# Decay tables on ScalarE, states ahead of masks, rows ahead of weights: three reorderings in a fused RWKV-5 and top-1 routing kernel

## The chip, the cores and the metric

The kernel runs on one core of a Trainium2 chip. A core has TensorE (PE, with its weight loads shown apart as PEld), VectorE (DVE), ScalarE (ACT), GpSimd (POOL) and SyncE (SP), which here only issues DMA transfers. The engines run side by side and wait for each other by semaphores; each works through its own instructions in order. The metric is the device time of one execution in microseconds (us). The kernel before takes 476.0 us in the median of three runs (474.22 to 477.74). The profile is of one execution with a span of 475.0 us.

## The reference

An attention block with a decaying state feeds a mixture of experts with one expert per token.

```python
# r, k, v: (4, 8, 768, 48); w, u: (8, 48)
for t in range(S):
    cur = einsum('bhd,bhe->bhde', u * k[t], v[t])
    y[t] = einsum('bhd,bhde->bhe', r[t], state + cur)
    state = w[:, :, None] * state + einsum('bhd,bhe->bhde', k[t], v[t])
x = y.transpose(0, 2, 1, 3).reshape(3072, 384)
logits = x @ w_gate                       # (3072, 8)
expert = argmax(logits); gate = softmax(logits)[expert]
for e in range(8):                        # w1: (384, 1024), w2: (1024, 384) per expert
    out[mask] = gate * (relu(x[mask] @ w1[e]) @ w2[e])
```

## The kernel before

The attention is cut into 32 units: 4 batches, 2 halves of 384 positions (3 chunks of 128), 4 pairs of heads. With Wp holding the rising powers of w within a chunk and Wr the falling ones, a unit scales r and k by tables (W1 and W2, shifted by half a chunk so that the numbers stay near 1), forms the products of a chunk, puts u's term on the diagonal, masks the part above it, and adds the term of the state that the chunks before left. The states come from k scaled by Wg and v.

The powers are doubled step by step on VectorE, after some matmuls that keep TensorE busy:

```python
        warm = pool.tile([128, 128], FP32, name="warm")
        for i in range(WARM):
            nc.tensor.matmul(warm, lhsT=ident, rhs=ident, start=True, stop=True, skip_group_check=True)

# ... (ranges of w, seven doublings of Wp and Wr on VectorE)
```

The tables and the scaling of a unit:

```python
        def tables(h0, h1):
            hs = slice(h0, h1)
            by = bc(w_64[:, hs, None], [128, h1 - h0, C])
            nc.vector.tensor_tensor(W2[:, hs], Wr[:, hs], by, op=ALU.mult)
            nc.vector.tensor_tensor(W1[:, hs], Wp[:, hs], by, op=ALU.mult)

        # tables_g(h0, h1): W3 = Wr * pw[LV-1] on VectorE, turned on TensorE, copied to Wg by ACT
# ...
        def u_scale(u):
            x = units[u]
            hp = x["hp"]
            nc.gpsimd.tensor_tensor(x["RK"], x["r"], x["k"], op=ALU.mult)
            nc.gpsimd.tensor_tensor(x["K"], x["k"], bc(W2[:, hp, None, :], [128, HC, C]), op=ALU.mult)
            nc.vector.tensor_tensor(x["R"], x["r"], bc(W1[:, hp, None, :], [128, HC, C]), op=ALU.mult)

        def u_scale_g(u):
            x = units[u]
            hp, ns = x["hp"], x["ns"]
            nc.gpsimd.tensor_tensor(
                x["Kg"][:, 0:ns, :], x["kt"][:, 0:ns, :],
                bc(Wg[:, hp].rearrange("p h d -> p (h d)")[:, None, :], [128, ns, 2 * D]), op=ALU.mult)

```

Products, diagonal, mask, states and output of a unit. Gp is one PSUM buffer for all units, P has two per head of the pair:

```python
        def u_scores(u):
            x = units[u]
            hp, A = x["hp"], x["A"]
            P = x["P"] = [ps.tile([128, 512], FP32, name=f"P{hi}", tag=f"P{hi}", bufs=2) for hi in range(2)]
            for c in range(HC):
                for hi in range(2):
                    q = slice(64 * hi, 64 * hi + D)
                    o = HC * C + c
                    nc.tensor.matmul(P[hi][:, o:o + 1], lhsT=x["RK"][q, c, :],
                                     rhs=wu[q, 1, hp:hp + 1], start=True, stop=True, skip_group_check=True)
            for c in range(HC):
                for hi in range(2):
                    q = slice(64 * hi, 64 * hi + D)
                    nc.tensor.matmul(P[hi][:, c * C:(c + 1) * C], lhsT=x["K"][q, c, :], rhs=x["R"][q, c, :],
                                     start=True, stop=True, skip_group_check=True)
            dv = ca.tile([128, 2, HC], FP32, name="dv", bufs=2)
            for hi in range(2):
                nc.scalar.copy(dv[:, hi], P[hi][:, HC * C:HC * C + HC])
            for c in range(HC):
                for hi in range(2):
                    nc.scalar.activation(A[:, hi, c, :], ident, func=ACT.Copy, scale=dv[:, hi, c:c + 1])

        def u_mask(u):
            x = units[u]
            A, P = x["A"], x["P"]
            for hi in range(2):
                nc.vector.copy_predicated(
                    A[:, hi], bc(mask[:, None, :].bitcast(I32), [128, HC, C]),
                    P[hi][:, 0:HC * C].rearrange("p (c t) -> p c t", t=C))
# ...
        def u_state(u):
            x = units[u]
            St, hp = x["St"], x["hp"]
            for c in range(x["ns"]):
                for hi in range(2):
                    nc.tensor.matmul(Gp[64 * hi:64 * hi + D, c, hi, 0:D], lhsT=x["Kg"][:, c, hi * D:(hi + 1) * D],
                                     rhs=vh(x, c, hi, D), start=True, stop=True, skip_group_check=True)
            prev = units[u - HP]["St"][:, HC - 1] if x["hf"] else None
            for c in range(x["ns"]):
                if prev is None:
                    nc.vector.tensor_copy(St[:, c, :, 0:D], Gp[:, c, :, 0:D])
                else:
                    nc.vector.scalar_tensor_tensor(out=St[:, c, :, 0:D], in0=prev[:, :, 0:D],
                                                   scalar=wC[:, hp:hp + 1], in1=Gp[:, c, :, 0:D], ...)
                prev = St[:, c]
        # ... u_out: yp = states x R (L533) + V x A (L537); y copied by ACT (L540)
```

u_gate turns a half's outputs into rows of x and their logits (three chunks per half, one in each of three units). choose makes gate weights and the expert of each row of a batch; its last steps store the rows to x_hbm in HBM, from the SP queue. ranks, onehots and early work out where each row goes; early does so ahead of time for two full tiles of 128 rows of experts 0 and 1. These steps are spread over units by a list:

```python
        for b in range(B - 1):
            g = 2 * HP * (b + 1) + 2
            for i in range(4):
                todo[g + min(i, 1) + i // 3].append(lambda b=b, i=i: chosen[b][i]())
            for i, step in enumerate(R.ranks(b, "y") + R.onehots(b, 3)):
                todo[g + 3 + i].append(step)
            if b == NB - 1:
                mark, columns, index = R.early("y")
                todo[g + 6].append(mark)
                todo[g + 7].append(columns)
                todo[g + 9].append(index)
        tiles = [Tile(R, j, early=True) for j in range(NEARLY)] + [Tile(R, j) for j in range(NSURE - NEARLY)]
```

The main program. Loads of r, k, v are issued four units ahead from the SP queue; the first four experts' second weights and two first weights are loaded beside the units. The buffers of the units lie in the memory of the last four experts' second weights, so those are loaded when the units end:

```python
            tables(0, 1)
            u_scale(0)
            tables_g(0, HP)
            u_scores(0)
            tables(1, HP)
            u_scale(1)
            u_scale_g(0)
            u_scores(1)
            u_mask(0)
            u_state(0)
            u_scale_g(1)
            R.begin()
            gate_weights()
            for u in range(NU):
                if u + 4 < NU:
                    u_load(u + 4)
                if HP <= u < HP + 4 * NW:
                    w2_load((u - HP) // 4, u % 4, 4)
                elif HP + 4 * NW <= u < HP + 4 * NW + NEARLY * DT:
                    tiles[(u - HP - 4 * NW) // DT].load_w1(wp, (u - HP - 4 * NW) % DT)
                if u + 2 < NU:
                    u_scale(u + 2)
                    u_scale_g(u + 2)
                if u + 1 < NU:
                    if u:
                        u_scores(u + 1)
                    u_mask(u + 1)
                    u_state(u + 1)
                u_out(u)
                if u >= HP and u % HP < HC:
                    u_gate(u // HP - 1, u % HP, "rw")
                for step in todo[u]:
                    step()
                # ... gather of the early tiles in unit 28
            fr.close()
            for e in range(NW, E):
                w2_load(e)
            t0, t1, t2, t3 = tiles[0:4]
            t0.turn(la, "g")
            # ... rows of x of the last three chunks
            mo = em.enter_context(tc.tile_pool(name="mo", bufs=2))
            shift, first, weight, rest = chosen[B - 1]
            shift()
            t0.hidden(mo, 0)
            first()
            weight()
            rest()
            for step in R.ranks(B - 1, "rw"):
                step()
            t0.hidden(mo, 1)
            R.bases(rt)
            R.slots(rt)
            for u in range(NU, NU + HP):
                for step in todo[u]:
                    step()
            for step in R.onehots(B - 1):
                step()
            R.owners(rt)
            t2.load_w1(wp)
            t1.turn(la, "g")
            t0.result(mo)
            R.index(rt, "rw")
            t2.load_x(mo)
            t3.load_x(mo)
            t0.store()
            t1.hidden(mo, 0)
            t1.hidden(mo, 1)
            t3.load_w1(wp)
            t1.result(mo)
            t1.store()
            t2.turn(mo, "g")
```

A tile gathers 128 rows by index (xs), turns them on TensorE (xTp, copied to xT), multiplies by w1 of its expert (hp, with relu to hT) and by w2 (yp), scales by the gate weight (yo) and stores by index:

```python
        def turn(self, mo, tag):

            p = self.R.ps.tile([128, DT, 128], FP32, name="xTp", tag=tag, bufs=BUFS[tag])
            for d in range(DT):
                nc.tensor.transpose(p[:, d, :], self.xs[:, 128 * d:128 * d + 128], ident)
            self.xT = self.tile(mo, [128, DT, 128], "xT", 2)
            nc.vector.tensor_copy(self.xT, p)
        # ... hidden: hp = w1 x xT, relu to hT; result: yp = hT x w2, yo = yp * xs[:, DM:W]
```

run_tiles repeats this for 26 tiles, with rows two tiles and weights two tiles ahead. A general path for other values of w exists in the file and does not run here.

## Time and profile before

| engine | busy us | share of the span |
|---|---|---|
| PE | 443.7 | 93% |
| PEld | 371.7 | 78% |
| DVE | 151.5 | 32% |
| ACT | 125.8 | 26% |
| POOL | 159.7 | 34% |

DMA moved 95.45 MB, 201 GB/s over the span. The page of the profile begins with these totals. Its second part cuts the span into 40 slices: a digit is the busy share of an engine in tenths (9 is 90% or more), PEclk is the granted TensorE clock in tenths of full speed, DMA the mean busy share of the core's 16 DMA engines. Further views list who waited for whom (engine, line, what it waited for; total us, times, longest), the instructions in order of time with the idle time of their engine before them in brackets, and the busy time in chosen stretches. L512 is line 512 of the kernel's file. A wait for several semaphores is put down to the one that came last by the profile; where the engine named had long been done, it was another. A matmul of 32-bit numbers appears as two records.

Lines to know: L480 and L485 the diagonal's and the chunk's products (P), L489 and L492 the diagonal on ACT, L498 the mask, L512 the state matmuls (Gp), L517 and L519 the state updates out of Gp, L533 and L537 the output (yp), L459, L460 and L461 the scaled RK, K and R, L466 the scaled k for the states, L566 the rows of x (rp), L163 the store of rows, L886 the gather of a tile, L892 and L894 its turning, L905 and L914 its two products.

### The profile page before, as it was taken

Reading aid. Unit: us, or ns where it says so; the run is one execution under the profiler, and the core shown is the slowest. Engines: PE = TensorE matmul, PEld = TensorE weight load, DVE = VectorE, ACT = ScalarE, POOL = GpSimd, SP = SyncE. Lnnn points to the kernel's source line nnn. Section 1 sums busy time; section 2 is a strip of 40 time slices with the busy share of each in tenths; the row PEclk is TensorE's granted clock in tenths of the full one; section 3 lists DMA queues with packets and bytes.
Section 4 is the critical chain, followed back from the end, with each engine's and each line's share of the span. In section 5 each row is a group of like instructions: output and inputs, shape, how many; then the busy total and the mean of one; then the engine's idle time right before and its main releaser. Section 6 shows DMA issues by size and latency. Waiting matters only on the chain.

```text
span 475.0 us, 10408 instructions
## 1 busy us (share of the span) xinstructions
PE 443.7 (93%) x4138; PEld 371.7 (78%) x4138; DVE 151.5 (32%) x399; ACT 125.8 (26%) x376; POOL 159.7 (34%) x193
## 2 busy tenths in 40 slices
PE   4999989889979996999999999999999999999992
PEld 4888888878868876877777888887777788888871
DVE  7436785985886720110001100001000010000100
ACT  0557776656555210111111111111111111111110
POOL 7857773964852025111111222111111112211000
PEclk8569999999989998999999999999999999999997
DMA  6348859949927997555555445445555544445400
GB/s 234 118 133 271 282 170 305 397 176 336 400 97 245 369 340 179 192 182 193 199 205 183 164 166 184 162 174 177 183 185 199 203 170 151 179 171 180 155 17 14
DMA packets 24576, 95.45 MB, mean 201 GB/s; under 512 B 3840, under 2 KB 6950, under 8 KB 20676
## 3 DMA queue, kind: packets, MB, share of 16 engines
q1 hardware_dynamic: 20322, 83.40, 49.6%
q0 software_dynamic: 3904, 11.23, 8.3%
q8 instruction: 38, 0.62, 0.6%
q14 instruction: 22, 0.18, 0.1%
q10 hardware_dynamic: 290, 0.02, 0.0%
HBM read 85.18 MB, written 10.24 MB: 201 GB/s over the span
## 4 chain that ended last, share of the span: by engine, by line
issue 35%; PE 31%; POOL 6%; DMA 3%; DVE 2%; POOLq 0%; ACT 0%
PE hp L905 13%; PE yp L914 10%; POOL xs L886 3%; DMA w_all<-in_r_k_units_dram 2%; POOL out_dram L919 2%; PE rp L566 2%; DMA xs<-x_hbm,idx 2%; PE yp L537 2%; PE yp L533 1%; PE P L485 1%; PE P L480 1%; PE xTp L892 1%; PE Gp L512 1%; POOL w_all L459 0%; POOL w_all L460 0%
## 5 line engine op out<-in xcount | busy, mean ns | idle before, releaser
L905 PEld LDWEIGHTS hp<-xT,w1s 128*128 128x128 f32 x1344 | 155.8, 193 | 8.5 <-DVE xT L894 1.7
L905 PE MATMUL hp<-xT,w1s 128*128 128x128 f32 x1344 | 156.7, 277 | 1.3 <-DVE xT L894 1.3
L914 PE MATMUL yp<-w_all,hT 128*128 (+1 forms) x448 | 149.1, 486 | 0.0
L914 PEld LDWEIGHTS yp<-w_all,hT 128*128 128x128 f32 x448 | 82.9, 190 | 51.9
L907 ACT ACTIVATE hT<-hp 128x512 f32<-128x512 f32 x56 | 33.4, 597 | 268.9 <-PE hp L905 267.4
L919 POOL DMA_INDIRECT out_dram<-yo,idx x26 | 26.5, 1019 | 224.2 <-DVE yo L916 214.7
L492 ACT ACTIVATE A<-ident,dv 128x128 f32<-128x128 f32 x192 | 59.6, 389 | 0.2 <-ACT dv L489 0.2
L894 DVE COPY xT<-xTp 128x384 f32<-128x384 f32 x28 | 15.6, 557 | 132.3 <-PE xTp L892 132.3
L916 DVE TENSOR_SCALAR yo<-yp,xs 128x384 f32<-128x384 f32 x26 | 16.1, 618 | 125.1 <-PE yp L914 125.1
L459 POOL TENSOR_TENSOR w_all<-w_all 128x384 f32<-128x384 f32 x32 | 35.1, 1098 | 32.3 <-PE rkp L716 11.1
L498 DVE COPY_PREDICATED A<-mask,P 128x384 f32<-128x384 int32 x64 | 33.8, 582 | 36.0 <-ACT A L492 24.2
L537 PE MATMUL yp<-A,w_all 128*64 128x128 f32 x384 | 42.1, 293 | 0.0
L886 POOL DMA_INDIRECT xs<-x_hbm,idx x26 | 25.3, 973 | 36.2 <-ACT hT L907 28.5
L460 POOL TENSOR_TENSOR w_all<-w_all,W 128x384 f32<-128x384 f32 x32 | 34.8, 1087 | 2.7 <-PE P L485 1.4
L533 PE MATMUL yp<-w_all,St 128*64 128x128 f32 x320 | 34.5, 291 | 0.0
L485 PE MATMUL P<-w_all 48*128 48x128 f32 x384 | 32.3, 305 | 1.7 <-DVE w_all L461 1.4
L480 PEld LDWEIGHTS P<-wu,w_all 48*128 48x128 f32 x384 | 26.4, 204 | 6.5 <-POOL w_all L459 2.3
L480 PE MATMUL P<-wu,w_all 48*128 48x1 f32 x384 | 28.9, 262 | 1.6 <-POOL w_all L459 1.6
L461 DVE TENSOR_TENSOR w_all<-w_all,W 128x384 f32<-128x384 f32 x32 | 27.6, 862 | 2.5 <-DMA w_all<-in_r_k_units_dram 2.4
L485 PEld LDWEIGHTS P<-w_all 48*128 48x128 f32 x384 | 26.7, 206 | 2.1 <-POOL w_all L460 1.6
L537 PEld LDWEIGHTS yp<-A,w_all 128*64 128x64 f32 x384 | 26.9, 149 | 0.4 <-DVE A L498 0.4
L466 POOL TENSOR_TENSOR w_all<-w_all,Wg 128x288 f32<-128x288 f32 (+1 forms) x32 | 25.2, 788 | 2.8 <-ACT Wg L438 1.4
(127 smaller groups left out, 254.4 us busy)
## 6 DMA issues: line engine op xcount, KB each, us to landing
w1s<-in_moe_w_dram SPq DMA_DIRECT2D x26, 1536.0 KB, 6.5
w_all<-in_r_k_units_dram SPq DMA_DIRECT2D x32, 384.0 KB, 5.8
w_all<-in_v_k_units_dram SPq DMA_DIRECT2D x32, 288.0 KB, 5.3
w_all<-in_moe_w_dram SPq DMA_DIRECT2D x16, 384.0 KB, 4.9
w_all<-in_moe_w_dram SPq DMA_DIRECT2D x4, 1536.0 KB, 7.9
w1s<-in_moe_w_dram SPq DMA_DIRECT2D x6, 512.0 KB, 8.6
x_hbm<-w_all SPq DMA_DIRECT2D x4, 577.5 KB, 4.6
x_hbm<-xb SPq DMA_DIRECT2D x4, 577.5 KB, 14.3
```

Source lines behind the costliest of these rows:

```text
L459: nc.gpsimd.tensor_tensor(x["RK"], x["r"], x["k"], op=ALU.mult)
L460: nc.gpsimd.tensor_tensor(x["K"], x["k"], bc(W2[:, hp, None, :], [128, HC, C]), op=ALU.mult)
L480: nc.tensor.matmul(P[hi][:, o:o + 1], lhsT=x["RK"][q, c, :], rhs=wu[q, 1, hp:hp + 1], start=True, stop=True, skip_group_check=True)
L485: nc.tensor.matmul(P[hi][:, c * C:(c + 1) * C], lhsT=x["K"][q, c, :], rhs=x["R"][q, c, :], start=True, stop=True, skip_group_check=True)
L492: nc.scalar.activation(A[:, hi, c, :], ident, func=ACT.Copy, scale=dv[:, hi, c:c + 1])
L498: nc.vector.copy_predicated(A[:, hi], bc(mask[:, None, :].bitcast(I32), [128, HC, C]), P[hi][:, 0:HC * C].rearrange("p (c t) -> p c t", t=C))
L533: nc.tensor.matmul(yp[q, c, :], lhsT=old[:, hi, :], rhs=x["R"][:, c, :], start=True, stop=False, skip_group_check=True)
L537: nc.tensor.matmul(yp[q, c, :], lhsT=vh(x, c, hi, 64), rhs=x["A"][:, hi, c, :], start=old is None, stop=True, skip_group_check=True)
L886: nc.gpsimd.indirect_dma_start(out=self.xs, out_offset=None, in_=x_hbm[:, :], in_offset=off)
L905: nc.tensor.matmul(p[:, f, :], lhsT=self.w1[:, d, o:o + 128], rhs=self.xT[:, d, :], start=d == 0, stop=d == DT - 1)
L914: nc.tensor.matmul(p, lhsT=self.hT[:, f, :], rhs=rhs, start=f == 0, stop=f == FT - 1)
L919: s_ = nc.gpsimd.indirect_dma_start(out=out[:, :], out_offset=bass.IndirectOffsetOnAxis(ap=self.idx, axis=0), in_=self.y[:, :], in_offset= ...
```

## The change

It has four parts. At the start, the decay tables are made by ACT, one pair of heads at a time, instead of by VectorE for several pairs at once; unit 0's K is scaled by VectorE; products come ahead of the diagonal's; ACT loads its function table at the very beginning; 18 warming matmuls stand in place of 9, with 6 and 4 further ones ("idle") between the first units; the setup of the routing and of IW moves from before the first unit to the third. In each unit, the states are worked out ahead of the mask. In the list of routing steps, ranks and one-hots come one unit earlier, early's steps are spread wider, and one of its reductions stands alone. At the passage to the tiles, the last batch's rows are stored ahead of the last four second weights, two of which are issued only after the gathers of the third and fourth tile; the second tile is turned earlier in the program and copied by ACT. What is computed stays the same. The aim is to start the units sooner and at full clock, to take the mask out of the way of Gp's release, and to have the rows in HBM in time for the first gathers.

The diff, with cuts (" ...") between its pieces:

```diff
 NW = E // 2
-WARM = 9
+WARM = 18
 BUFS = dict(P0=2, P1=2, y=2, g=1, rw=1)
 ...
+    wake = consts.tile([1, 1], FP32, name="wake")
+    nc.scalar.copy(wake, ident[0:1, 0:1])
     with tc.tile_pool(name="pw", bufs=1, space=PSUM) as pool:
 ...
         Gp = ps.tile([128, HC, 2, 64], FP32, name="Gp", tag="g", bufs=1)
-        nc.vector.memset(Gp, 0.0)
 ...
-        def tables(h0, h1):
-            hs = slice(h0, h1)
-            by = bc(w_64[:, hs, None], [128, h1 - h0, C])
-            nc.vector.tensor_tensor(W2[:, hs], Wr[:, hs], by, op=ALU.mult)
-            nc.vector.tensor_tensor(W1[:, hs], Wp[:, hs], by, op=ALU.mult)
 ...
-        def tables_g(h0, h1):
-            hs = slice(h0, h1)
-            n = h1 - h0
-            W3 = As[2].rearrange("p h c t -> p (h c t)")[:, 0:HP * C].rearrange("p (a t) -> p a t", a=HP)
-            nc.vector.tensor_tensor(W3[:, hs], Wr[:, hs], bc(pw[:, LV - 1, hs, None], [128, n, C]), op=ALU.mult)
+        W3 = As[2].rearrange("p h c t -> p (h c t)")[:, 0:HP * C].rearrange("p (a t) -> p a t", a=HP)
 ...
+        def scaled(out, tab, hp, by):
+            nc.scalar.activation(out[:, hp, :], tab[:, hp, :], func=ACT.Copy, scale=by[:, hp:hp + 1])
 ...
+        def tables(hp):
+            scaled(W2, Wr, hp, w_64)
+            scaled(W1, Wp, hp, w_64)
 ...
+        def table_g():
             w3p = ps.tile([128, HP, C], FP32, name="w3p", tag="rw", bufs=1)
-            for hp in range(h0, h1):
+            for hp in range(HP):
                 nc.tensor.transpose(w3p[:, hp, :], W3[:, hp, :], ident)
-            nc.scalar.copy(Wg[:, hs], w3p[:, hs].rearrange("p a (h d) -> p a h d", h=2)[:, :, :, 0:D])
+            nc.scalar.copy(Wg, w3p.rearrange("p a (h d) -> p a h d", h=2)[:, :, :, 0:D])
 ...
+        def idle(n):
 ...
+            warm = ps.tile([128, 128], FP32, name="warm", tag="y", bufs=2)
+            for i in range(n):
+                nc.tensor.matmul(warm, lhsT=ident, rhs=ident, start=True, stop=True, skip_group_check=True)
 ...
-        def u_scale(u):
+        def u_scale(u, eng=nc.gpsimd):
             x = units[u]
             hp = x["hp"]
-            nc.gpsimd.tensor_tensor(x["RK"], x["r"], x["k"], op=ALU.mult)
-            nc.gpsimd.tensor_tensor(x["K"], x["k"], bc(W2[:, hp, None, :], [128, HC, C]), op=ALU.mult)
+            if u:
+                nc.gpsimd.tensor_tensor(x["RK"], x["r"], x["k"], op=ALU.mult)
+            eng.tensor_tensor(x["K"], x["k"], bc(W2[:, hp, None, :], [128, HC, C]), op=ALU.mult)
             nc.vector.tensor_tensor(x["R"], x["r"], bc(W1[:, hp, None, :], [128, HC, C]), op=ALU.mult)
+            if u == 0:
+                nc.gpsimd.tensor_tensor(x["RK"], x["r"], x["k"], op=ALU.mult)
 ...
-        def u_scores(u):
 ...
+        def u_own(u):
 ...
             x = units[u]
-            hp, A = x["hp"], x["A"]
-            P = x["P"] = [ps.tile([128, 512], FP32, name=f"P{hi}", tag=f"P{hi}", bufs=2) for hi in range(2)]
+            hp, P = x["hp"], x["P"]
             for c in range(HC):
 ...
+        def u_products(u):
 ...
+            x = units[u]
+            P = x["P"]
             for c in range(HC):
 ...
+        def u_diagonal(u):
+            x = units[u]
+            A, P = x["A"], x["P"]
             dv = ca.tile([128, 2, HC], FP32, name="dv", bufs=2)
 ...
+        def u_scores(u, parts=(u_own, u_products, u_diagonal)):
+            units[u]["P"] = [ps.tile([128, 512], FP32, name=f"P{hi}", tag=f"P{hi}", bufs=2) for hi in range(2)]
+            for part in parts:
+                part(u)
 ...
             for i, step in enumerate(R.ranks(b, "y") + R.onehots(b, 3)):
-                todo[g + 3 + i].append(step)
+                todo[g + 2 + i].append(step)
             if b == NB - 1:
-                mark, columns, index = R.early("y")
-                todo[g + 6].append(mark)
-                todo[g + 7].append(columns)
-                todo[g + 9].append(index)
+                for step, i in zip(R.early("y"), (5, 6, 9, 11)):
+                    todo[g + i].append(step)
         tiles = [Tile(R, j, early=True) for j in range(NEARLY)] + [Tile(R, j) for j in range(NSURE - NEARLY)]
 ...
         with tc.manual_schedule():
-            tables(0, 1)
-            u_scale(0)
-            tables_g(0, HP)
-            u_scores(0)
-            tables(1, HP)
+            tables(0)
+            u_scale(0, nc.vector)
+            tables(1)
+            for hp in range(HP):
+                scaled(W3, Wr, hp, pw[:, LV - 1])
+            u_scores(0, (u_products, u_own))
+            table_g()
+            u_diagonal(0)
             u_scale(1)
+            nc.vector.memset(Gp, 0.0)
+            tables(2)
+            tables(3)
+            idle(6)
+            u_scores(1, (u_products, u_own, u_diagonal))
             u_scale_g(0)
-            u_scores(1)
+            u_scale_g(1)
+            idle(4)
+            u_state(0)
             u_mask(0)
-            u_state(0)
-            u_scale_g(1)
-            R.begin()
-            gate_weights()
             for u in range(NU):
 ...
                         u_scores(u + 1)
+                    u_state(u + 1)
                     u_mask(u + 1)
-                    u_state(u + 1)
                 u_out(u)
+                if u == 2:
+                    R.begin()
+                    gate_weights()
                 if u >= HP and u % HP < HC:
 ...
             fr.close()
-            for e in range(NW, E):
-                w2_load(e)
             t0, t1, t2, t3 = tiles[0:4]
 ...
             rest()
+            w2_load(NW)
+            w2_load(NW + 1)
             for step in R.ranks(B - 1, "rw"):
 ...
             t0.hidden(mo, 1)
+            t1.turn(la, "g", nc.scalar.copy)
             R.bases(rt)
 ...
             t2.load_w1(wp)
-            t1.turn(la, "g")
             t0.result(mo)
 ...
             t0.store()
+            for e in range(NW + 2, E):
+                w2_load(e)
             t1.hidden(mo, 0)
 ...
                 nc.scalar.activation(Bv[:, :, 1, :], sel, func=ACT.Copy, scale=lo_f)
-                nc.vector.tensor_reduce(self.isA[:, 0:nb * G], sel, axis=AX, op=ALU.add)
 ...
+            def taken():
+                nc.vector.tensor_reduce(self.isA[:, 0:nb * G], sel, axis=AX, op=ALU.add)
 ...
             lt = sel = Bv = None
-            return [mark, columns, index]
+            return [mark, columns, index, taken]
 ...
-        def turn(self, mo, tag):
+        def turn(self, mo, tag, copy=nc.vector.tensor_copy):
 ...
             self.xT = self.tile(mo, [128, DT, 128], "xT", 2)
-            nc.vector.tensor_copy(self.xT, p)
+            copy(self.xT, p)
```

## The prediction

> **What bounds the kernel now.** I read the page's slices first, to split the span into stages. Each column is one fortieth of it, 11.9 us.
>
> ```profile
> PE   4999989889979996999999999999999999999992
> PEclk8569999999989998999999999999999999999997
> DMA  6348859949927997555555445445555544445400
> ```
>
> Up to column 13 (about 153 us) 32 attention units run, from column 15 on the expert tiles. The tiles keep TensorE full: the chain of waits shows one tile as 5.36 (hp) + 0.33 (xTp) + 5.16 (yp) = 10.85 us, again and again from 190 to 467 us. Nothing there is changed, so all that can be won lies before 190 us. There the weak spots are the clock in columns 2 and 3, the PE digits 7 and 6 around columns 12 and 16, and a DMA row that swings between 9 and 2.
>
> One-microsecond stretches of the start come next. The columns are: stretch, length, busy time of PE, PEld, DVE, ACT and POOL with instruction counts, granted clock, DMA share, GB/s.
>
> ```profile
> 8.00:9.00 1.00, 0.00 (x0) 0.00 (x0) 1.00 (x2) 0.00 (x0) 1.00 (x2) 0.93 1.05 412
> 9.00:10.00 1.00, 0.00 (x0) 0.00 (x0) 1.00 (x1) 0.00 (x0) 0.69 (x1) 0.50 1.01 400
> ...
> 31.00:32.00 1.00, 1.00 (x12) 1.00 (x12) 0.07 (x1) 1.00 (x5) 0.84 (x2) 0.50 0.07 16
> 32.00:33.00 1.00, 1.00 (x14) 0.68 (x10) 1.00 (x3) 0.21 (x2) 0.00 (x0) 0.62 0.00 0
> 33.00:34.00 1.00, 1.00 (x20) 1.00 (x22) 0.93 (x4) 0.46 (x1) 0.19 (x1) 1.00 0.05 14
> ```
>
> The nine warming matmuls end at 5.8 us, PE has nothing until the transposes at 10.4 us, the clock falls to 0.50 just before 9 us and comes back only at 32.4 us. For 23 us the first units run at half speed, while PE is the busiest engine.
>
> Then the waits of PE inside the units, which the list of who waited for whom gives as:
>
> ```profile
> PE Gp L512 <- POOL w_all L459: 3.6, 5, 1.2
> PE Gp L512 <- POOL w_all L460: 3.2, 3, 1.7
> PE Gp L512 <- issue: 1.7, 1, 1.7
> ```
>
> POOL is named, but neither line writes what Gp reads. The timeline around the longest such wait shows who ends last (start, length, instruction, idle time before it):
>
> ```profile
> 136.93 1.05 DVE L498 COPY_PREDICATED A<-mask,P 128x384 f32<-128x384 int32 x2 [1.49 <-ACT A L492]
> 137.87 0.65 DVE L519 SCALAR_TENSOR_TENSOR St<-St,pw,Gp 128x96 f32<-128x96 f32 x2
> ...
> 138.63 0.56 PE L512 MATMUL Gp<-w_all 128*48 128x48 f32 x8 [1.72 <-issue]
> ```
>
> VectorE waits for ACT's diagonals, masks, and only then empties the single Gp buffer, at 138.52; PE starts 0.11 us later. I checked the waits at 53.55, 69.17, 93.70 and 102.97 us the same way: each ends some 0.1 us after the last L519 or L517/L519 pair.
>
> Last, the passage from units to tiles:
>
> ```profile
> 157.95 1.60 SPq L163 DMA_DIRECT2D x_hbm<-xb  x2
> 168.08 5.62 PE L905 MATMUL hp<-xT,w1s 128*128 128x128 f32 x48 [0.69 <-DVE xT L894]
> 174.36 0.99 POOL L886 DMA_INDIRECT xs<-x_hbm,idx  x1 [28.54 <-ACT hT L907]
> 181.94 0.52 PE L892 MATMUL xTp<-ident,xs 128*128 128x128 f32 x3 [3.07 <-DMA xs<-x_hbm,idx]
> 183.11 7.16 PE L905 MATMUL hp<-xT,w1s 128*128 128x128 f32 x48 [0.65 <-DVE xT L894]
> ```
>
> The index is ready at 169.2 us (the timeline's L764), yet the gather goes out only at 174.4: it waits for the rows issued at 157.95, which took up to 15.2 us to land behind 6 MB of second weights. PE runs dry at 178.9, and the next tile takes 7.16 us for 5.36 because the clock has dropped again.
>
> **What the Trainium skill says.** *TensorE: Matmul & The Clock Gate*, "What's actually happening": the PE clock is gated to half after an idle window of about 3.4 us and released after a busy one. The trace agrees with the fall (idle from 5.8, half by 9.0) and with the recoveries at 138.5 to 141.9 and 183.0 to 186.4 us, 3.4 us each; it disagrees between 12 and 32 us, where PE shows as nearly full and stays at half. I take from this that keeping the clock is cheaper than winning it back. *SBUF — State Buffer*, "Who interferes with whom": a DVE instruction with two SBUF inputs blocks against GpSimd reads, and ACT waits for nobody. L461 shows it, 0.56 us in the median and 1.25 at 7.59 beside POOL. *ScalarE: Activation LUTs*, "What ACT_TABLE_LOAD costs": a load takes about 1.28 us; here it is 1.28 us at 11.56, right ahead of the Wg copy. *DMA: Bandwidth & Descriptors*, "Queues, rings and completion order": descriptors of a ring are consumed in order. That fits rows landing after weights queued ahead of them.
>
> **The change, part by part.**
>
> *Start.* Wr and Wp are done at 5.95 + 0.41 = 6.36 us. In the kernel before, VectorE then does a memset, two small tables, R(0), the 1.48 us table for Wg and the rest, and K(0) sits on POOL; the products of unit 0 start at 12.64. After it, ACT makes the two tables of pair 0 (a 128x128 scaled copy is 0.39 us, six in a row 1.86, so 0.31 each): ready at about 7.1. VectorE does K(0) and R(0), two at 0.56 to 1.25: about 8.5. So products start some 4 us earlier. Six more ACT copies end near 9.1, four transposes take about 0.9, the Wg copy 0.48 (table load gone): about 11. Diagonals 0.23 + 1.86 bring ACT to 13.1, mask 1.05 to 14.2. On the other side Kg of two units on POOL, 1.55, ends at 12.6, then Gp(0), St(0) 0.9, Gp(1) behind it in the one buffer. I put the first yp at 16.5 us, against 19.17: 2.7 us.
>
> *Clock.* Nine more warm matmuls at 0.44 us cold or 0.22 warm carry PE from 5.8 to between 7.8 and 9.8 us; products, transposes and the six and four idle matmuls (10 x 0.22 = 2.2 us, in time that PE would wait anyway) leave no hole near 3.4 us. At full clock the stretch from the first yp to the sixth unit's Gp (41.87 us before) is 1.33 (yp) + 1.54 (P) for the first, 3.25 for each of three units without rp and 3.9 for one with it: 2.9 + 9.75 + 3.9 = 16.5 us. That puts it at 33.0 us: 8.9 us won in all.
>
> *States ahead of masks.* After this, L517/L519 follow Gp at once instead of the mask, which comes 2.1 us (0.23 + 1.86) after the products plus 1.05 of its own. The mask is still 0.4 us or more ahead of its yp. From Gp(6) on the waits are 0.55 + 1.16 + 0.35 + 1.68 + 0.52 + 0.82 + 1.72 = 6.8 us. The half clock from 138.5 to 141.9 follows from the last of them: 3.4 us for 1.7 of work, 1.7 more. Sum 8.5. I give 1.5 back to loads (rival two): 7.0. Spreading the routing steps to other units is part of this; I give it nothing of its own.
>
> *Rows ahead of weights.* PE lost 0.69 at t1's xT (now copied by ACT, which is free there), then from 178.87 to 183.11 instead of the usual 0.33 + 0.6 or so, 3.3 us, then 1.8 for the half clock: 5.8. The rows (1.2 MB, 3 us at 400 GB/s) now start with an idle ring at about the same point, land within some 6 us, long before the index. Two weights follow, then t2's w1, then the last two weights with the gather beside them: the gather is issued 5 us earlier and may take 5 to 7 us. I count 5.5.
>
> Sum: 8.9 + 7.0 + 5.5 = 21.4; 476.0 - 21.4 = 454.6, so **455 us**.
>
> **Rivals.** *One, the clock does not hold.* The gap between the last warm matmul and the first product, or the waits for Wg, close the clock again, and the mix of small matmuls fails to reopen it, as from 12 to 32 us. For it: those 20 us. Against: after 33 us the same mix, with holes of 1.7 us, keeps full clock until 138 us. Then the start brings 3 instead of 8.9: 461 us. *Two, the loads become the bound.* Eight units need 8 x (384 + 288 + 384) KB and two row stores, 9.8 MB, 24.6 us at 400 GB/s, against 30 us of PE. But the sync queue stands still at the row stores (17.5 + 12.1 us in its waits, for the reciprocal on VectorE), and DMA is empty at 100 to 104 us, then full until 132. PE waits of 0.5 to 0.9 us on r,k data appear right after; faster units would lengthen them. Then the middle brings 2 to 3: 459 us. *Three, the gather is late anyway*, now against w1 and the last two weights (4.7 MB, 12 us from about the same moment), or PE's clock falls in a shorter hole. Then the end brings 2: 458 us. All three at once would leave some 469.
>
> **Range and chances.** The parts lie in different stages and hardly trade against each other, except that a faster start loads the DMA rings harder. Each rival costs 3.5 to 6 us, I give each about one in four, and the start could be better by 2 to 3 than my chain. So 448 to 463 in 8 of 10. Two per cent needs 9.5 us, less than half the sum: faster 0.95, same 0.04, slower 0.01.
>
> **What would show it.** Right: granted clock 1.00 from about 8 us on, with the first yp near 16 us; no Gp waits of over 0.3 us; no half clock around the fourth batch's start; the units' last Gp near 132 us (148.3 before); the third tile's xTp right behind the second's yp; 10.85 us per tile as before. Wrong: half clock between 9 and 30 us; L487 or L497 waiting on r,k loads for several us; a wait of xTp for the gather. What would overthrow the whole: a tile stage longer than 10.85 us a tile, from weights that come late for the last experts.

## The result, and the profile after

The changed kernel takes **457.9 us** (median of four runs, 457.38 to 458.53); the kernel before takes 475.1 in the median of its four. The ratio is 0.963, 95% interval 0.959 to 0.968. The profiled execution is 456.2 us long (475.0 before). The prediction said 455, between 448 and 463.

Line numbers have moved: L466/L467/L468 are the products RK, K and R of the next unit (L459 to L461 before), L487 and L497 are P's own column and P's products (L480, L485), L533 is Gp, L165 the row stores, L597 the second weights, L900 w1, L918 the gathers, L937 hp and L946 yp of the tiles. The slices of the page, each 11.4 us now:

```profile
PE   7899998998999988999999999999999999999993
PEclk9999998998999999999999999999999999999999
DMA  7488859869743999644555555555544544555400
```

The clock row has lost its 5 and 6 in columns 2 and 3. Two 8s are new, in columns 7 and 10, each with a dent in PE at the same place. DMA still swings.

The start, by one-microsecond stretches (columns as before):

```profile
8.00:9.00 1.00, 0.55 (x5) 0.35 (x4) 1.00 (x2) 0.94 (x4) 1.00 (x2) 1.00 1.01 400
9.00:10.00 1.00, 0.92 (x17) 0.95 (x18) 1.00 (x1) 0.00 (x0) 0.80 (x1) 1.00 0.97 356
31.00:32.00 1.00, 1.00 (x24) 0.87 (x20) 0.77 (x2) 1.00 (x4) 1.00 (x2) 1.00 0.95 335
```

The granted clock is 1.00 where it was 0.50, and between 31 and 32 us PE does 24 matmuls where it did 12. The first yp starts at 17.12 us, the Gp that the prediction follows at 33.23 (41.87 before).

In the middle the list of waits has no Gp left. Two other waits are there, and the sync queue's own list tells where they come from (total, times, longest):

```profile
PE P L487 <- POOL w_all L466: 3.4, 2, 1.9
```

```profile
SPq L165 <- DVE xb L182: 22.2, 2, 15.3
SPq L165 <- DVE w_all L182: 13.3, 2, 6.8
```

L182 is the reciprocal that the row stores wait for. How a wait of the queue becomes a wait of PE can be followed through one batch, in stretches of the middle (granted clock, DMA share and GB/s are last) and in the timelines of POOL and PE:

```profile
57.00:62.00 5.00, 5.00 (x93) 4.66 (x91) 4.72 (x14) 4.53 (x16) 3.39 (x5) 1.00 0.03 12
67.00:72.00 5.00, 5.00 (x102) 4.75 (x100) 2.38 (x9) 3.98 (x16) 2.75 (x3) 1.00 1.04 316
72.00:76.00 4.00, 2.37 (x32) 2.04 (x30) 2.62 (x7) 1.24 (x5) 3.20 (x3) 0.90 1.03 400
76.00:79.40 3.40, 3.40 (x52) 3.18 (x50) 2.51 (x6) 2.36 (x9) 3.28 (x4) 0.61 1.04 402
...
66.63 1.39 POOL L466 TENSOR_TENSOR w_all<-w_all 128x384 f32<-128x384 f32 x1 [6.14 <-DMA w_all<-in_r_k_units_dram]
74.03 0.83 PE L487 MATMUL P<-wu,w_all 48*128 48x1 f32 x12 [1.50 <-POOL w_all L466]
```

The queue issues nothing from 54.3 to 61.2 us, so DMA is empty at 57 to 62; the loads behind the store then come all at once and fill it. POOL waits 6.14 us for r,k data, until 66.6, PE waits 1.50 us for POOL, until 74.0, and from 76.0 on PE runs at a mean clock of 0.61 for 3.4 us. The same follows the next batch, with a wait of 1.93 us until 107.6.

Last, the passage to the tiles, in the timelines of the sync queue, GpSimd and PE:

```profile
143.40 0.89 SPq L165 DMA_DIRECT2D x_hbm<-xb  x2
...
154.82 0.99 POOL L918 DMA_INDIRECT xs<-x_hbm,idx  x1 [22.16 <-PE hp L937]
...
163.31 0.49 PE L924 MATMUL xTp<-ident,xs 128*128 128x128 f32 x3
164.65 5.62 PE L937 MATMUL hp<-xT,w1s 128*128 128x128 f32 x48 [0.85 <-DVE xT L926]
170.11 0.49 PE L924 MATMUL xTp<-ident,xs 128*128 128x128 f32 x3
171.01 2.82 PE L946 MATMUL yp<-w_all,hT 128*128 x8 [0.41 <-issue]
175.01 2.85 PE L946 MATMUL yp<-w_all,hT 128*128 x8 [1.18 <-ACT hT L939]
```

Rows, gather and transposes follow as intended. New is the third tile's yp: it comes in two halves of eight, late, and ends 2.1 us later than 16 matmuls at 0.33 us would. From there a tile takes 10.85 us, as before.

The account, from these starts of PE instructions:

| stretch | before | after | won |
|---|---|---|---|
| to the Gp at the end of the start | 41.87 | 33.23 | 8.6 |
| from there to the last Gp | 106.41 | 100.52 | 5.9 |
| from there to the end of the third tile's hp | 41.99 | 36.52 | 5.5 |
| the third tile's yp | | | -2.1 |
| behind the last matmul | | | 0.9 |
| profiled span | 475.0 | 456.2 | 18.8 |

### The profile page after: what moved, and what is told of

The parts are those of the page before. It is cut to its first block, busy times and chain, and to the rows that moved or that the text cites. A ratio compares the mean times of both kernels' runs of the same rounds, so it can differ in the third digit from the quotient of the medians.

```text
span 456.2 us, 10424 instructions
## 1 busy us (share of the span) xinstructions
PE 439.0 (96%) x4176; PEld 368.0 (81%) x4176; DVE 147.1 (32%) x394; ACT 129.2 (28%) x390; POOL 158.2 (35%) x192
## 4 chain that ended last, share of the span: by engine, by line
PE 51%; issue 36%; POOL 6%; DMA 2%; another core or an unknown queue 1%; DVE 1%; ACT 1%; POOLq 0%; SPq 0%; ACTq 0%; DVEq 0%
PE hp L937 13%; PE yp L946 12%; PE P L497 5%; PE yp L558 5%; PE P L487 5%; PE yp L554 4%; PE rp L587 4%; POOL xs L918 3%; PE Gp L533 2%; DMA w_all<-in_r_k_units_dram 2%; POOL out_dram L951 2%; PE xTp L924 1%; PE warm L444 1%; POOL w_all L467 0%
## 5 line engine op out<-in xcount | busy, mean ns | idle before, releaser
L937 PEld LDWEIGHTS hp<-xT,w1s 128*128 128x128 f32 x1344 | 154.3, 192 | 7.8 <-DVE xT L926 1.1
L937 PE MATMUL hp<-xT,w1s 128*128 128x128 f32 x1344 | 155.1, 275 | 0.8 <-DVE xT L926 0.8
L946 PE MATMUL yp<-w_all,hT 128*128 (+1 forms) x448 | 149.5, 487 | 1.6 <-ACT hT L939 1.2
L946 PEld LDWEIGHTS yp<-w_all,hT 128*128 128x128 f32 x448 | 82.9, 190 | 54.1 <-ACT hT L939 1.8
L926 DVE COPY xT<-xTp 128x384 f32<-128x384 f32 x27 | 15.1, 557 | 132.2 <-PE xTp L924 122.4
L466 POOL TENSOR_TENSOR w_all<-w_all 128x384 f32<-128x384 f32 x31 | 34.8, 1123 | 27.2 <-DMA w_all<-in_r_k_units_dram 9.9
L558 PE MATMUL yp<-A,w_all 128*64 128x128 f32 x384 | 40.5, 282 | 0.1
L918 POOL DMA_INDIRECT xs<-x_hbm,idx x26 | 25.3, 974 | 29.8 <-PE hp L937 22.5
L554 PE MATMUL yp<-w_all,St 128*64 128x128 f32 x320 | 33.5, 282 | 0.0
L467 POOL TENSOR_TENSOR w_all<-w_all,W 128x384 f32<-128x384 f32 x31 | 33.2, 1071 | 0.0
L497 PE MATMUL P<-w_all 48*128 48x128 f32 x384 | 30.0, 289 | 0.8 <-DVE w_all L468 0.5
L487 PEld LDWEIGHTS P<-wu,w_all 48*128 48x128 f32 x384 | 24.0, 187 | 7.4 <-POOL w_all L466 3.9
L487 PE MATMUL P<-wu,w_all 48*128 48x1 f32 x384 | 26.5, 249 | 3.4 <-POOL w_all L466 3.4
L468 DVE TENSOR_TENSOR w_all<-w_all,W 128x384 f32<-128x384 f32 x32 | 25.3, 794 | 5.6 <-DMA w_all<-in_r_k_units_dram 4.8
L497 PEld LDWEIGHTS P<-w_all 48*128 48x128 f32 x384 | 24.5, 191 | 1.2 <-issue 0.7
```

What stands on the lines that cost most here:

```text
L487: nc.tensor.matmul(P[hi][:, o:o + 1], lhsT=x["RK"][q, c, :], rhs=wu[q, 1, hp:hp + 1], start=True, stop=True, skip_group_check=True)
L554: nc.tensor.matmul(yp[q, c, :], lhsT=old[:, hi, :], rhs=x["R"][:, c, :], start=True, stop=False, skip_group_check=True)
L558: nc.tensor.matmul(yp[q, c, :], lhsT=vh(x, c, hi, 64), rhs=x["A"][:, hi, c, :], start=old is None, stop=True, skip_group_check=True)
L918: nc.gpsimd.indirect_dma_start(out=self.xs, out_offset=None, in_=x_hbm[:, :], in_offset=off)
L937: nc.tensor.matmul(p[:, f, :], lhsT=self.w1[:, d, o:o + 128], rhs=self.xT[:, d, :], start=d == 0, stop=d == DT - 1)
L946: nc.tensor.matmul(p, lhsT=self.hT[:, f, :], rhs=rhs, start=f == 0, stop=f == FT - 1)
```

## The experiments

The theory: the change has done what it was made for; what it fell short by is rival two (stores hold up loads), and a wait of the third tile for second weights that land late. Against it stand the rivals named with each run. Ratios are to the kernel before, run beside each group. The times are medians of all runs of a kernel; the ratios leave out the runs that were over 1.5% slower than its fastest.

| kernel | us | ratio, 95% interval |
|---|---|---|
| the change | 457.9 | 0.963, 0.959 to 0.968 |
| late_store | 452.0 | 0.951, 0.949 to 0.954 |
| two_ahead | 461.6 | 0.972, 0.969 to 0.974 |
| both | 454.4 | 0.956, 0.953 to 0.960 |
| weights_ahead | 464.2 | 0.978, 0.974 to 0.982 |
| three | 449.7 | 0.946, 0.943 to 0.950 |
| three_again (the same) | 450.1 | 0.945, 0.942 to 0.949 |
| late_xl | 451.7 | 0.949, 0.946 to 0.953 |
| cold | 464.0 | 0.975, 0.970 to 0.980 |
| warm_only | 475.6 | 0.999, 0.996 to 1.001 |
| masks_first | 464.8 | 0.977, 0.972 to 0.982 |
| states_only | 472.8 | 0.991, 0.989 to 0.994 |
| before_late | 473.5 | 0.996, 0.993 to 0.999 |

### Row stores later (late_store)

```
-            store_rows(b, xb, 0, HC)           # at the end of weight()
+ return [..., lambda: store_rows(b, xb, 0, HC), lambda: store_rows(b, xb, HC, G)]
-            for i in range(4):
-                todo[g + min(i, 1) + i // 3].append(...)
+            for i, d in enumerate((0, 1, 1, 3, 4)):
+                todo[g + d].append(...)
```

> The kernel after, but the two row stores of each of the first three batches stand two unit boundaries later in the sync queue (half 0 at the fourth unit after the batch, half 1 at the fifth, instead of second and third). Bytes, waits and all other work are the same. Theory (rival two of the prediction: the queue stands still at a store whose row weights are not ready, so DMA runs empty, and the r,k loads behind it come late): the waits SPq L165 <- DVE xb (22.2 us) and <- DVE w_all (13.3 us) shrink to a few us except at the last batch, DMA no longer falls to 0 near 57 to 61 us, PE's waits for POOL L466 (1.50 us at 74.0 and 1.93 us at 107.6) go, and with them the two windows of half clock behind them (3.4 us each, 1.7 us of work lost each): 3.4 + 3.4 = 6.8 us, so about 451 us against 458. Rival theory (the loads of these units are limited by DMA bandwidth, wherever the stores stand): the waits move to other units and the time stays at 456 to 458 us. Third: the later stores hold the one buffer of rows longer and stop other work: slower than 458.

452.0 us. Two of the stretches above, with the empty DMA and with the lowered clock, in this kernel, then its whole middle, and last the middle of the kernel after:

```profile
57.00:62.00 5.00, 5.00 (x93) 4.67 (x91) 4.72 (x14) 4.51 (x16) 3.37 (x4) 1.00 0.90 287
76.00:79.40 3.40, 3.40 (x68) 3.15 (x66) 2.96 (x8) 2.43 (x10) 2.37 (x4) 1.00 1.03 396
33.27:126.84 93.57, 93.57 (x1741) 86.81 (x1741) 81.45 (x211) 68.96 (x248) 71.16 (x76) 1.00 0.90 304
```

```profile
33.23:133.75 100.52, 96.80 (x1739) 89.58 (x1738) 79.71 (x213) 69.37 (x248) 71.19 (x76) 0.97 0.82 284
```

DMA is busy again at 57 us, PE has no hole at all in 93.57 us, and the clock stays up. The middle of the kernel after is 6.95 us longer: PE is idle for 3.72 of them, and its busy time is 3.23 longer, which fits two windows of half clock. The order in the queue was the bound, not bandwidth. Of the five profiles of this kind (the kernel after with late stores), four have a middle of 93.2 to 93.9 us. The fifth, three_again below, takes 96.2: its clock falls to half from about 90.3 to 93.7 us, though PE has no hole over 0.26 us.

### The same edit in the kernel before (before_late)

The diff is the same, against the kernel before.

> The kernel before, with the one edit that brought 6.0 us to the kernel after: row stores of the first three batches two unit boundaries later. Theory (in the kernel before PE's holes were the masks' and the loads had some slack, so that the queue's stop at the stores cost little; only the faster units of the kernel after turned it into a bound): 472 to 475 us, a gain of 3 at most (PE's waits at P L480 for POOL L459, 1.6 us, and at most a part of the others). Rival (the stores cost the same in both kernels, so that the change did not create this wait): about 469 us.

473.5 us, in the range of the theory, and 0.7 under the 474.3 us of the kernel before beside it. In its profile the middle takes 103.2 us instead of 106.4: 3.2 us, against 6.95 after the change, which fits faster units making a small wait into a larger one. Even the 3.2 is hardly seen in the time. In the same profile the passage, from the last Gp to the end of the third tile's hp, takes 44.87 us instead of 41.99: PE waits 4.83 us for the third tile's gather, not 3.07.

### States ahead of masks, alone and undone (states_only, masks_first)

```
                     if u:
                         u_scores(u + 1)
-                    u_mask(u + 1)
                     u_state(u + 1)
+                    u_mask(u + 1)
```

in the kernel before (states_only), and the reverse in the kernel after (masks_first).

> The kernel before with the states ahead of the masks on VectorE from the second unit on, and nothing else of the change. Theory (the masks cost PE its holes at Gp from the sixth unit on; what is left is the loads' share): between the sixth and the last unit's Gp PE's waits at Gp go and waits at P for POOL's L459 come or grow; this stretch takes 100 to 102 us instead of 106.4; 468 to 471 us in all. Rival (the loads are the bound in the kernel before as well): 473 to 475. Rival (states ahead does it all): below 466.

472.8 us, less than expected: the middle takes 104.2 us, not 100 to 102. PE's waits at Gp are gone there as well, but waits at P have come for them (old line numbers):

```profile
PE P L480 <- POOL w_all L459: 4.4, 3, 2.5
```

> The kernel after, but from the second unit on the mask is queued ahead of the states on VectorE again, as in the kernel before. Theory (the mask waits 2.1 us for ACT's diagonals and holds the states, and PE waits for them): waits of PE at Gp come back in most units, 6 to 8 us in sum, some of it in the place of the two waits for POOL L466 (3.4 us) and their half clock: 462 to 465 us. Rival (the loads, held at the row stores, are the bound of these units now, and slower units only use up that wait): 458 to 460 us.

464.8 us, the middle 107.2. Its list of PE's waits, from 20 to 150 us, has both kinds:

```profile
PE Gp L533 <- POOL w_all L466: 3.6, 4, 1.2
PE P L487 <- POOL w_all L466: 2.9, 2, 1.8
PE Gp L533 <- issue: 1.5, 1, 1.5
```

Put together, the middle in us: masks first with early stores 106.4, with late stores 103.2; states first with early stores 104.2 (alone) and 100.5 (in the whole change), with late stores 93.6. Either cure alone brings 2 to 3 us, as the other bound takes over; with both the middle is 12.8 us shorter, though the kernel with both has the rest of the change too. States ahead brings 2.2 us alone and 5.9 with the rest of the change. PE's idle time in the middle falls by 4.9 us in the first case (10.41 to 5.55) and by 6.7 in the second (to 3.72), but its busy time grows, by 2.7 and by 0.8 us: both kernels have two windows of half clock where the kernel before has one. Why the two differ beyond that stays open; the spread routing steps and the other start lie between them, and each figure is of one profile.

### The clock at the start (cold, warm_only)

```
-WARM = 18
+WARM = 9
-            idle(6)
-            idle(4)
```

in the kernel after (cold), and only `WARM = 18` in the kernel before (warm_only).

> The kernel after, with 9 instead of 18 warm matmuls and without the 6 and 4 idle ones of the first units; tables, orders and all else stay. It leaves out only matmuls whose results nobody reads. Theory (of the 8.6 us won up to the sixth unit, some 2 are from the shorter chain to the first products and some 6 from a full clock between 9 and 33 us): PE falls to half clock between about 6 and 9 us and stays there until well after 20 us: sixth unit's Gp at 36 to 40 us instead of 33.2, and the whole at 461 to 465 us against 458. Rival (the other order alone, with products sooner behind the warm matmuls and denser, keeps or regains the clock): within 1 us of 458.

464.0 us, inside the range, but not by that path: the sixth unit's Gp starts at 35.29 us, 2.1 later than after and earlier than expected. The products between 9 and 20 us in cold, then in the kernel after (min, median, max ns), and a stretch of cold:

```profile
L497 PE MATMUL P<-w_all x24: 417/418/579, 9.3 to 14.3; 48*128 48x128 f32 x24
```

```profile
L497 PE MATMUL P<-w_all x34: 272/272/373, 9.1 to 20.0; 48*128 48x128 f32 x34
```

```profile
10.00:11.00 1.00, 1.00 (x14) 1.00 (x13) 0.84 (x2) 0.00 (x0) 0.05 (x1) 1.00 0.82 242
```

Without the extra matmuls a product takes half as long again, and PE's other matmuls are slow too until 20.8 us, so PE did slow down; yet the column of the granted clock shows 1.00. In the kernel before the same products take 417 ns at a shown clock of 0.50. The other losses against the kernel after lie behind the start: 2.5 us in the middle, where the waits at P are 4.6 instead of 3.4 us, and some 0.8 in the passage.

> The kernel before with 18 instead of 9 warm matmuls, and nothing else. Theory (it is the hole between the last warm matmul and the first products, at 12.6 us, that costs the clock; the warm matmuls now end near 8.5 us, which leaves a hole of some 4 us, and the sparse units behind it do not win it back): half clock from 12.6 to about 20 to 32 us as before, 472 to 476 us. Rival (more warm matmuls alone keep the clock, the order matters little): full clock at 12.6 us, sixth unit's Gp near 36 us instead of 41.9, 468 to 470 us.

475.6 us, no difference: PE ends its warm matmuls at 8.2 us, stands idle for 3.83, has 0.97 us of work from 9 to 13, and runs at 0.5 until past 30 us. More matmuls alone bring nothing; a hole stays behind them, of 3.83 us here, of 3.30 in cold and of 0.54 in the kernel after. The order alone (cold) has the full clock back by 20.8 us; with both, no profile lost it before the sixth unit's Gp. How much of the 8.6 us the order owns can't be told to a microsecond: four profiles with the old start (before, before_late, states_only, warm_only) reach that Gp 40.1, 36.1, 36.8 and 40.8 us after their first warm matmul, since the clock comes back at different moments (states_only also has its other order of states by then; undoing that order in masks_first costs 1.7 us up to this Gp). With the whole new start, eight profiles reach it 31.4 to 31.7 us after it: the held clock also takes out the chance.

### Weights and rows in the passage (weights_ahead, two_ahead)

All four second weights ahead of the rows:

```
+            for e in range(NW, E):
+                w2_load(e)
             t0, t1, t2, t3 = tiles[0:4]
```

and both later places taken out; in two_ahead only the first two are moved.

> The kernel after, but all four second weights (6.3 MB, about 16 us at the 400 GB/s that this stretch shows) stand ahead of the rows of the last batch, as in the kernel before; this undoes the third part of the change and leaves the rest. By the prediction's step (rows behind weights cost 5.5 us): about 462 to 463 us. By what the trace of after shows (the memory of these weights is free at 137.7 us, 6 us before the rows are issued, DMA is empty until then, and all second weights have landed before the first yp that must wait for them): rows land at about 156 to 158 us, just behind the gather's issue at 154.8, the gather is some 2 us later at most and still ahead of its transposes at 163, and the stall of t2's result goes: 455 to 457 us. In that case it was the wait for the weights' memory in the kernel before (queue stopped until 152.7 us), and not the order as such, that cost the time.

464.2 us: my expectation fell, and the prediction's step stands. GpSimd and PE in this kernel (its lines of the tiles stand two lower):

```profile
159.39 0.99 POOL L916 DMA_INDIRECT xs<-x_hbm,idx  x1 [26.50 <-ACT hT L937]
...
167.39 0.87 PE L922 MATMUL xTp<-ident,xs 128*128 128x128 f32 x3 [4.24 <-DMA xs<-x_hbm,idx]
```

The weights were issued from 132.5 us on, the rows at 143.1, and still the gather could start only at 159.4, 4.6 us later than in the kernel after, then beside t2's w1. PE waits 4.24 us and then runs at half clock until about 173 us (hp takes 7.64 us). *DMA: Bandwidth & Descriptors* of the Trainium skill, "Queues, rings and completion order", says that a ring's descriptors are consumed in order; this run agrees: with 6.3 MB ahead of them the row stores take up to 15.1 us to land, against 8.6 in the kernel after. The weights did start early, but DMA was still full with them when the rows were issued (a share of 0.95 and more from 140 us on). In this profile the passage up to the third tile's hp takes 43.08 us, 6.6 more than in the kernel after, while the third tile's yp runs without its stall.

> The kernel after, but the first two of the four second weights (1.5 MB each) go into the sync queue ahead of the rows of the last batch; the other two stay where they are. DMA was empty from 132 to 144 us in the kernel after, and the last reader of their memory ends at 137.7 us, so they should run from about 138 to 146 us. Theory (the first yp of an expert chosen at run time waits for every second weight, and the last two landed at 170.3 us because DMA was full from 144 to 175 us): 3 MB less in that stretch, the last two land some 7 us earlier, t2's yp follows its hp within 0.4 us, and the stall of about 2.1 us in t2's result goes; holes of some 0.8 us between 162 and 168 us may go too: 455 to 456 us. Rival (the stall comes from something else, such as the tile's transposes or the copies on ACT and VectorE that were held until 174.4 us): the stall stays, 458 us. Rival from the prediction (rows must be ahead of weights): rows land 3 to 7 us later, the gather with them: no gain or up to 3 us slower, 458 to 461.

461.6 us, slower, for a reason none of the three had. The stall went, as PE's sequencer shows. Its semaphore waits at L946 between 155 and 180 us (min, median, max ns) in the kernel after, then in two_ahead:

```profile
L946 PEldq EVENT_SEMAPHORE  x3: 51/51/1556, 169.2 to 169.4; - x3
```

```profile
L946 PEldq EVENT_SEMAPHORE  x3: 51/51/51, 169.9 to 170.1; - x3
```

This is the third tile's yp, the first whose expert is chosen at run time, and it waits 1.56 us before it issues. With two weights earlier it doesn't. But PE, the sync queue and GpSimd go on:

```profile
171.00 37.84 SPq L900 DMA_DIRECT2D w1s<-in_moe_w_dram  x4
...
172.73 0.94 POOL L918 DMA_INDIRECT xs<-x_hbm,idx  x1 [0.30 <-issue]
...
184.67 0.52 PE L924 MATMUL xTp<-ident,xs 128*128 128x128 f32 x3 [2.86 <-DMA xs<-x_hbm,idx]
185.21 7.05 PE L946 MATMUL yp<-w_all,hT 128*128 x16
```

In the kernel after, the next w1 load (1.5 MB) went out only at 174.35, at the end of the stall and behind the fifth tile's gather at 172.03. Here that load goes out first, at 171.0, the gather lands 11.8 us after its issue, PE waits 2.86 us, and half clock costs 1.7 more (7.05 us for a yp of 5.33).

### All together (both, three, three_again, late_xl)

> Later row stores in the first three batches and two second weights ahead of the last rows. If both theories hold, the two parts lie in different stages and add: 6.8 + 2.3 = 9.1 us, 449 us. If the loads are bound by bandwidth: 455 to 456. If the stall of t2's result has another cause: 451. If neither: 458.

454.4 us: the first part adds, the second takes back 2.5 against late_store, by a wait of 3.84 us for the same gather. That gather stands behind five gathers for tiles that may not be needed, which are ready just as early. The third part moves those:

```
-            late = late_rows(R, NSURE - NEARLY, rt)
-            run_tiles(tiles[2:], wp, mo)
+            late = []
+            run_tiles(tiles[2:], wp, mo, lambda: late.extend(late_rows(...)))
     # in run_tiles, behind the load_x of the fourth tile of its list: between()
```

> Later row stores, two second weights ahead of the last rows, and in addition the five gathers of rows for tiles that may not be needed (xl, one after the other on GpSimd, 6.3 us in the queue) moved from ahead of the gather for the fifth tile (xs) to three tiles later. Theory: in the kernel with the first two parts (454.4 us) PE waits 3.84 us for that xs gather (issued 164.7, landed 177.6 us), because the five xl gathers and a w1 load of 1.5 MB stand ahead of it in a full DMA, and a window of half clock follows that loses 1.8 us more. With the xl gathers out of the way it is issued some 6 us earlier and ahead of that w1 load: no wait, no half clock: 454.4 - 5.6 = 449 us, which is better than later stores alone (452.0). Rival (DMA is full anyway between 150 and 178 us, whatever the order): the wait shrinks only by the bytes of the five gathers, 1 MB or 2.5 us at 400 GB/s: 451 to 452. Second rival: the xl gathers disturb a later tile, 452 or more.

449.7 us. GpSimd and PE in this kernel:

```profile
158.97 0.99 POOL L918 DMA_INDIRECT xs<-x_hbm,idx  x1 [0.30 <-issue]
...
163.36 0.49 PE L924 MATMUL xTp<-ident,xs 128*128 128x128 f32 x3
163.69 5.33 PE L946 MATMUL yp<-w_all,hT 128*128 x16
168.85 5.52 PE L937 MATMUL hp<-xT,w1s 128*128 128x128 f32 x48
174.21 0.49 PE L924 MATMUL xTp<-ident,xs 128*128 128x128 f32 x3
```

The gather goes out 5.75 us earlier than in the kernel with both parts (164.72), and PE runs from tile to tile without a hole.

> The kernel with later row stores, two second weights ahead of the last rows and the xl gathers three tiles later, beside the one that lacks the second part: 450 us, as before (449.65).

> Later row stores and the five xl gathers three tiles later, but the four second weights stay behind the last rows as in the kernel after. Theory (t2's result waits for the last second weights, whose bytes and place are unchanged): the stall of about 2 us in t2's result stays, only the wait of 0.63 us for the next xs gather goes: 451 to 452 us, 1.5 to 2 slower than with the two weights ahead as well. Rival (the 1 MB of the xl gathers is what makes the last weights late): they land 2.5 us earlier, the stall goes, and the time equals the kernel with all three parts, about 450.

450.1 and 451.7 us, run side by side: ratios 0.945 and 0.949, whose intervals overlap, so the times alone don't tell the two apart. The traces do: from the last Gp to the sixth tile's transposes it is 58.03 us with the two weights ahead, in both profiles, and 59.65 without, and PE's sequencer waits again, between 155 and 180 us of late_xl:

```profile
L946 PEldq EVENT_SEMAPHORE  x3: 51/51/2524, 162.1 to 162.3; - x3
```

So the weights' place makes the stall, not the bytes of the five gathers. The version with all three parts beats the kernel before by 5.4% and the changed kernel by some 8 us.

## Why the prediction was right, and where its steps were off

- **Start and clock, 8.9 us: 8.6.** First yp at 17.12 us for 16.5, the Gp at 33.23 for 33.0, clock 1.00 throughout. The chain of the new start was right, and the clock is shown; the size owes something to luck. Counted from the first warm matmul, the kernel after takes 31.4 us to this Gp, and the four profiles with the old start 36.1 to 40.8: the forecast was made from one near the top (40.1), and the same new start would have won as little as 4.7 or as much as 9.4. The reason is shared: without the extra matmuls, cold still took only 33.5.
- **States ahead of masks, 7.0: 5.9.** The Gp waits went, as did the half clock at the fourth batch. The mis-sized term is what is given back to the loads: 8.5 - 5.9 = 2.6 instead of 1.5. PE's idle time fell by 6.7 us, close to the 6.8 that were forecast; the 1.7 for the clock did not come, since two windows of half clock took the place of one and the busy time grew by 0.8. Rival two came true in part, by the mechanism it names: L487 waits for POOL's product, which waits for loads behind a stopped queue. The half clock behind each such wait was not in its price, and it was half of it: 3.23 of 6.95 us lost.
- **Rows ahead of weights, 5.5: 5.5 up to the third tile's hp**, and undoing it cost 6.2 us. The match to a tenth is luck here too: the same passage takes 43.8 to 44.9 us in three other profiles with the old order (warm_only, states_only, before_late), against 41.99 in the kernel before. Rival three, a gather late anyway, did not occur for the third tile.
- **Missing: 2.1 us in the third tile's yp.** The prediction placed the last two weights beside the gather and asked only whether the gather would be late, not who would wait for the weights. It named late weights as what could overthrow the whole, for the last experts; it was the first tile with a chosen expert that met them. That its wait is for the second weights is shown by two_ahead, three and late_xl. Why the second half of that yp waits another 1.18 us, for a copy on ACT that starts only at 174.4 although its hp ended at 170.3, is not settled; VectorE's next copy and the next w1 load start at the same moment.
- **Sum.** 8.6 + 5.9 + 5.5 - 2.1 + 0.9 (behind the last matmul, not traced further) = 18.8 in the profiles; 17.2 between the medians. Of the forecast 21.4 the profiles show 2.6 less: -0.3, -1.1 and -2.1 in the parts, and the 0.9 that nobody forecast. The other 1.6 is the difference between the profiled execution of the kernel before (476.7 us of device time) and its median, 475.1.

## What to carry to other kernels

A store in an in-order queue that waits for a late value stops every load behind it; place it where its value is surely ready, and do so before speeding up what consumes the loads. When a stall is taken away, look at what it was holding back: here it had kept a large load out of the way of a small gather. Price a PE hole of 1.5 us together with the half clock that may follow it. And before matching a forecast to a tenth of a microsecond, see how far profiles of nearly the same code lie apart: here 4.7 us in the start and 2.9 in the passage.

## What the runs showed of the hardware

- The granted clock of the profile can read 1.00 while PE is slow (cold, 9 to 15 us: 418 ns for a product that takes 272). The duration of a known matmul is the better witness.
- With the old start, PE wins its clock back at 22.1 us (before_late), 26.8 (states_only), 32.8 (before; the prediction read 32.4) or 33.5 (warm_only), though these starts differ in a few instructions only.
- Holes of 1.50 and 1.93 us in a stretch of small matmuls were each followed by 3.4 us of half clock, while one of 1.68 us in the kernel before (until 102.97 us) and one of 1.61 in weights_ahead (until 74.17) were not. In three_again 3.4 us of half clock came with no hole over 0.26 us. So the hole alone does not decide it.
- PE's sequencer waited 1.56 us (after) and 2.52 us (late_xl) on a semaphore, where the idle time of the same matmul is put down to "issue" alone, with 0.41 and 1.39 us.
